# Attention and a gated feed-forward on one core: other planner constants, and the last stores on two queues

## The chip, the core and the metric

The kernel runs on one core of a Trainium2 chip. The time is the device time of one execution in microseconds, given as the median of several runs; a profile is one execution taken by the hardware profiler. Times in the profile count from the start of its span.

## The reference

```python
scores = (1 / sqrt(64)) * q @ k.T                 # q, k, v: 8 batches, 12 heads, 448 rows, 64 columns
attn = exp(scores - max(scores)); attn = attn / (sum(attn) + 1e-9)
x = (attn @ v) as 3584 x 768                      # heads side by side
h = x @ w_in                                      # 768 x 2048
out = (h * sigmoid(h)) @ w_out                    # 2048 x 768, float32
```

## The kernel before

**Stages and names.** The work is in 16-bit floats with float32 sums in PSUM. Heads are taken in groups of four, three groups to a batch. A *unit* is one group with all its queries; in batch 0 each group makes two units of half the queries (224 columns, units 0 to 5), and from batch 1 on there are units 6 to 26 with 448 columns. In the profile the tiles have these names:

- `rk`, `rq`, `V`: keys, queries and values as they are loaded on GpSimd's queue; `KT`, `QT`: transposed by VectorE (lines 285, 296).
- `s`: scores, one *burst* for each quarter of the keys (line 311). A matmul of a burst has 32 rows, so that the four heads run in four row groups of TensorE. A burst fills two PSUM tiles (heads 0 and 1, heads 2 and 3); there are only two such tiles, tag `s`. Units 7 on come in pairs (7 and 8, 9 and 10, ...), whose last quarters share a burst of 16.
- `E`: the exp of the scores on ScalarE (line 348), two instructions to a burst. `T`: sums of E over key quarters on VectorE (line 359), an add that shortens the sums of weights.
- `a`: three products with E for each unit (line 375): part 0, the sums of weights, with `ones`; parts 1 and 2, with `V`. They run in column groups.
- `sT`, `inv`, `rdn`: transpose, reciprocal and spread of the sums of weights on VectorE (lines 415, 421, 424); `xT`: the normalized output (line 432), which is the input x of the feed-forward.
- `h`: x times one of the 16 blocks of w_in (line 446); `th`: tanh on ScalarE (line 457); `G` and `X`: (tanh + 1) times h on VectorE (line 493), the gated values.
- `o`: four plain products with w_out for the first two row tiles (line 551). `p`: all other products with w_out (line 537), as 13 *quads*: two row tiles by two halves of the inner dimension by two halves of the columns, in seven products in place of eight. They need sums of G (`S`, and G itself, line 527), sums of w_out (`D1`, `D4`, `D6` and two written into `w_out_t`, line 483), and sums of the results, read from PSUM by ScalarE copies and VectorE adds (lines 590 to 604, tiles `s`, `m`, `ost`).
- `z`: products of zeros that keep TensorE at work while it waits at the start (line 1148).

The tiles a, h, o, p and z share four PSUM banks, tag `m`: each product holds its bank until what reads it is done (sT for part 0, xT for parts 1 and 2, G for h, copies and adds for o and p).

**What sets the order.** Nothing is left to the compiler. The kernel carries a planner (class `Order`, line 89 on) that steps through a modelled time, with modelled costs of each instruction and counters for buffers (`Ring`), and writes down in which order each engine gets its instructions. ScalarE and VectorE take, of what is ready, the instruction with the least (ready time + bias); the biases are the numbers that stand in each `Op` (-2 for tanh, -1 for the gate, -10 for the sums' inverse, 8 for S, 20 for the transposes of k and q, 100 for the sums of w_out). TensorE chooses in the main loop: a score burst if it can run and either `PACE` modelled microseconds have gone by since the last, or no product of the list `moe` (h, o, p) is ready, or that list has fewer than 6 entries; otherwise a product of the list, otherwise a part of a. The planner's times only give the order; on the chip each engine runs its instructions in that order, each waiting for its inputs by semaphores.

Units 0 to 5 issue each burst as two halves of 8 matmuls, one for each pair of heads (the tuple `split`, line 964).

**Stores.** `store` (line 575) writes an output tile of 128 x 384 with four DMAs of 32 rows. They are issued by SP; only for the last quad (`4 * qd + 4 == NT * B`) and its tiles (0,0) and (1,1) the two odd ones are issued on ScalarE's queue.

Of the kernel before, what the change touches and what calls it, by code (L numbers as in the profile page):

```python
# [164 lines left out]
def kernel(  # L165
# [25 lines left out]
    NDC = DM // 128  # L191
    NT = 2 * S // 128
    OH = DM // 2
    PACE = 3
    LONE = NG + 1
    PIECES = ((0, 7), (7, TPP))
    NE, NXT = 9, 16
# [377 lines left out]
    def store(qd, i, j):  # L575
        u, t = divmod(2 * qd + i, NT)
        for w in range(4):
            r, col = divmod(128 * t + 32 * w, S)
            b = 2 * u + r
            dst = out[b * S : (b + 1) * S, OH * j : OH * (j + 1)].rearrange(  # L580
                "(i g) m -> g i m", g=TPP
            )

            eng = nc.scalar if w % 2 and 4 * qd + 4 == NT * B and i == j else nc.sync
            eng.dma_start(
                out=dst[col // 32], in_=ost_t[(qd, i, j)][32 * w : 32 * (w + 1), :]
            )
# [143 lines left out]
    moe = []  # L731
# [7 lines left out]
    def queue_ffn1(b, g0, g1):  # L739
        t0, t1 = 32 * g0, 32 * g1  # L740
        for f in range(NFF) if b == 0 else [x for f in range(HF) for x in (f, f + HF)]:

            def run(f=f):
                op = Op("PE", NDC * mm(t1 - t0), lambda: ffn1(b, f, t0, t1), tail=PE_OUT)
                if warm["on"]:
                    warm["on"] = False
                    m_ring.give(od.now)
                m_ring.take()
                od.on_pe(op, "full")
                th = od.add(  # L750
                    Op("ACT", act(t1 - t0), lambda: tanh(b, f, t0, t1), [op], -2, tail=0.2, ring=th_ring)
                )
                g = Op(
                    "DVE",
                    (t1 - t0) / 960.0 + 0.13,
                    lambda: gate(b, f, t0, t1),
                    [th],
                    -1,
                    then=lambda at: (m_ring.give(at), th_ring.give(at)),
                )  # L760
                g_op.setdefault((b, f), []).append(od.add(g))
                ffn1_left[b] -= 1

            def deps(f=f):
                made = [(x_op[(b, cc, g0)], cc * mm(t1 - t0)) for cc in range(NDC)] + ld_win[f]

                u, r = divmod(b, 2)
                for qd in range(NT * B // 4) if u else ():
                    if any(t // NT == u - 1 and (r or t % NT < 4) for t in (2 * qd, 2 * qd + 1)):
                        made += (  # L770
                            [plain_op.get(x) for x in ((0, 0), (0, 1), (1, 0), (1, 1))]
                            if qd == 0
                            else [pr_op.get((qd, m)) for m in (3, 4, 6, 7)]
                        )
                return made

            moe.append((deps, 1, run))
            ffn1_left[b] += 1

    def sums_w(ms):  # L780

        for m in ms:
            w_op[m] = [
                od.add(
                    Op(
                        "DVE",
                        0.9,
                        lambda m=m, f0=f0: combine_w(m, f0, f0 + 4),
                        ld_wout[0] + ld_wout[1] + list(plain_op.values()) * (m in (3, 7)),
                        100,  # L790
                    )
                )
                for f0 in (0, 4)
            ]

    def queue_plain(t, j):
        def run():
            op = Op("PE", NFF * mm(OH), lambda: plain(t, j), tail=PE_OUT)
            m_ring.take()
            od.on_pe(op, "full")  # L800
            plain_op[(t, j)] = op
            od.add(
                Op(
                    "ACT",
                    act(OH),
                    lambda: take_plain(t, j),
                    [op],
                    -0.3,
                    then=lambda at: (m_ring.give(at), ost_ring.give(at + STORED)),
                    ring=ost_ring,  # L810
                )
            )
            if len(plain_op) == 4:
                sums_w((3, 7))

        def deps():
            if any(len(g_op.get((0, f), ())) < len(PIECES) for f in range(NFF)):
                return [None]
            return ld_wout[j] + [(x, f * mm(OH)) for f in range(NFF) for x in g_op[(0, f)]]

        moe.append((deps, 1, run))
# [37 lines left out]
    def queue_quad(qd):  # L859
        quads.append(qd)  # L860
        took = {}

        def read(m, eng, fn, deps, *free):
            busy = act(OH) if eng == "ACT" else OH / 960.0 + 0.13
            bias = -0.3 if eng == "ACT" else -1
            ring = tmp_ring[m] if m in tmp_ring else ost_ring if m in (2, 5, 6, 7) else None

            def then(at):
                for r in free:
                    r.give(at)  # L870
                if ring is ost_ring:
                    ring.give(at + STORED)

            took[m] = od.add(Op(eng, busy, lambda: fn(qd), deps, bias, then=then, ring=ring))

        def queue(m, first):
            def run():
                op = Op("PE", HF * mm(OH), lambda: product(qd, m), tail=PE_OUT)
                if BANK[m] == m:
                    m_ring.take()  # L880
                if m in (5, 2, 1):
                    op.then = sg_ring.give
                od.on_pe(op, "full")
                pr_op[(qd, m)] = op
                if m == 3:
                    read(3, "ACT", take_3, [op])
                elif m == 4:
                    read(4, "DVE", take_4, [op, took[3]])
                elif m == 5:
                    read(5, "ACT", take_5, [op], m_ring)  # L890
                elif m == 2:
                    read(2, "ACT", take_2, [op], m_ring)
                elif m == 1:
                    read(1, "DVE", take_1, [op, took[4]])
                    read("less_12", "DVE", less_12, [took[1], took[5]])
                    read("less_21", "DVE", less_21, [took[1], took[2]])
                elif m == 6:
                    read(6, "DVE", take_6, [op, took["less_21"]], m_ring, tmp_ring[1])
                else:
                    read(7, "DVE", take_7, [op, took["less_12"]], m_ring, tmp_ring[3])  # L900

            def deps():
                made = list(w_op.get(m, [None])) + [x for y in first if y for x in [took.get(y)]]
                if m in (3, 4):
                    t = 2 * qd + m - 3
                    for b in {(128 * t + c) // S for c in (0, 127)}:
                        for f in range(HF):
                            x = g_op.get((b, f + HF * (m - 3)), [None])
                            made += [(y, f * mm(OH)) for y in x]
                    return made + ld_wout[0] + ld_wout[1]  # L910
                if m in (1, 6, 7):
                    made += [pr_op.get((qd, x)) for x in ((5, 2) if m == 1 else (1,))]
                x = sg_op.get((qd, m), [None, None])
                return made + [x[0], (x[1], 4 * mm(OH))]

            moe.append((deps, 1 if BANK[m] == m else 0, run))


        for m, first in ((3, ()), (4, (3,)), (5, (3,)), (2, (4,)), (1, ()), (6, ()), (7, (1,))):
            queue(m, first)  # L920
# [40 lines left out]
    qk_seq, av_seq = [], []  # L961
    for ns in jobs:
        if len(ns) == 1:
            split = ((0,), (1,)) if ns[0] < 6 else ((0, 1),)
            qk_seq += [(ns, c, ys) for c in range(NCH // per_burst(ns[0])) for ys in split]
        else:
            qk_seq += [([n], c, (0, 1)) for n in ns for c in range(NCH - 1)]
            qk_seq.append((ns, 3, (0, 1)))
        av_seq += [(ns, part) for part in range(3)]
# [139 lines left out]
    def after_av(n, part, op, nq):  # L1109
        b, hg, g0, g1 = units[n]  # L1110
        if part == 0:
            made = []
            before = ([op] + inv_op[-1:], [], norm_op[-4:])
            for step, busy in enumerate((nq / 960.0 + 0.15, 0.2, nq / 960.0 + 0.15)):
# [2 lines left out]
                    busy,  # L1117
                    lambda step=step: inverse(n, step),
                    made[-1:] + before[step],
                    -10,  # L1120
                )
                made.append(od.add(r))
            made[0].then = m_ring.give
# [29 lines left out]
    while True:  # L1153
# [4 lines left out]
        if od.free["PE"] <= od.now:  # L1158
# [6 lines left out]
                moe_i, moe_next = moe_ready(0)  # L1165
                soon.append(min([x for x in m_ring.free if x>od.now] or [od.now+0.1]))
            if qk is not None and qk <= od.now and (
                od.now >= pace["next"] or moe_i is None or len(moe) < 6
            ):
                u0 = units[qk_seq[0][0][0]]  # L1170
                pace["next"] = min(max(pace["next"], od.now - 4), od.now) + PACE * len(qk_seq[0][2]) / 2
                run_qk()
                od.now, keep = od.free["PE"], od.now
                while (a := av_at()) is not None and a <= od.now:
# [58 lines left out]
```

The softmax here doesn't subtract the row's maximum and nothing guards it: scores larger than these inputs give would overflow.

## Time and profile before

| what | value |
|---|---|
| median of 7 runs | 405.27 us (404.99 to 405.65) |
| profiled execution | 404.76 us, span 403.0 us |
| TensorE (PE) busy | 394.5 us, 98% |
| VectorE (DVE) busy | 299.3 us, 74% |
| ScalarE (ACT) busy | 233.8 us, 58% |
| GpSimd (POOL) busy | 95.9 us, 24% |
| granted TensorE clock | 0.999 |
| start of PE's last product | 395.74 us |

"Busy" adds the time of an engine's instructions. A row of the timeline gives the start, the length, the engine, the line and operation, the tiles as out<-in with their sizes, and the number of instructions merged; in brackets the idle time before it and what ended it. In the list of waits the three numbers are the microseconds in total, the number of waits and the longest. SPq and ACTq are the queues' own instructions, the issuing of DMAs.

### The profile page before, as it was taken

How to read it: one execution, taken by the hardware profiler on the slowest of the kernel's cores; microseconds unless marked ns; L12 is line 12 of the kernel's file. 1: busy time of each engine (PE TensorE's matmuls, PEld its weight loads, DVE VectorE, ACT ScalarE, POOL GpSimd, SP SyncE). 2: the span in 40 equal slices, each digit the busy share in tenths (PEclk: the TensorE clock that was granted, in tenths of full speed). 3: DMA queues.
4: the chain of work that ended last, by engine and by line, in shares of the span. 5: the costliest groups of instructions: out<-in, count | busy, mean ns of one | idle time of the engine just before them, and what ended most of it. 6: DMA issues, size and time to landing. Idle time of an engine off the chain costs nothing.

```text
span 403.0 us, 9442 instructions
## 1 busy us (share of the span) xinstructions
PE 394.5 (98%) x3767; PEld 203.3 (50%) x3767; DVE 299.3 (74%) x646; ACT 233.8 (58%) x360; POOL 95.9 (24%) x175
## 2 busy tenths in 40 slices
PE   8999999999999999999999999999999999999994
PEld 7676754444444444444455444443445444655562
DVE  2555676999979797696788678788698677674763
ACT  3887895796566866545961495764971573224410
POOL 6775383724003415120000630530000000000000
PEclk9999999999999999999999999999999999999999
DMA  7999999967015936392002782642002300131024
GB/s 110 175 166 206 196 135 218 182 85 116 2 45 100 172 50 81 58 172 56 0 2 62 124 144 38 92 88 62 1 21 53 88 0 2 35 81 44 2 49 107
DMA packets 38747, 34.43 MB, mean 85 GB/s; under 512 B 11952, under 2 KB 37936, under 8 KB 38704
## 3 DMA queue, kind: packets, MB, share of 16 engines
q0 software_dynamic: 27952, 22.82, 39.2%
q1 hardware_dynamic: 10560, 10.83, 10.4%
q8 instruction: 29, 0.48, 0.5%
q10 hardware_dynamic: 192, 0.20, 0.2%
q14 instruction: 14, 0.11, 0.1%
HBM read 45.61 MB, written 11.01 MB: 141 GB/s over the span
## 4 chain that ended last, share of the span: by engine, by line
PE 96%; DVE 1%; ACT 1%; issue 0%; ACTq 0%
PE h L446 38%; PE p L537 30%; PE s L311 12%; PE a L375 11%; PE o L551 3%; PE z L1148 2%; ACT E L348 1%; DVE T L359 1%; DVE rdn L424 0%; DVE ost L590 0%; DVE sT L415 0%; DVE G L493 0%; DVE X L493 0%; DVE inv L421 0%; DVE ones L212 0%
## 5 line engine op out<-in xcount | busy, mean ns | idle before, releaser
L348 ACT ACTIVATE E<-s 128x896 f16<-128x896 f32 (+1 forms) x172 | 149.2, 915 | 47.8 <-PE s L311 46.5
L446 PE MATMUL h<-xT,w_in_t 128*128 128x448 f16 (+1 forms) x864 | 157.8, 332 | 0.1
L446 PEld LDWEIGHTS <-w_in_t 128*128 128x128 f16 x864 | 79.2, 98 | 72.6 <-issue 19.8
L457 ACT ACTIVATE th<-h 128x448 f16<-128x448 f32 (+1 forms) x144 | 71.7, 505 | 58.1 <-PE h L446 53.4
L493 DVE SCALAR_TENSOR_TENSOR G<-th,h 128x448 f16<-128x448 f16 (+2 forms) x144 | 74.8, 532 | 35.2 <-ACT th L457 33.3
L250 POOL DMA_DIRECT2D V<-in_v_dram x88 | 48.6, 566 | 127.9 <-PE a L375 104.2
L311 PE MATMUL s<-QT,KT 32*128 32x448 f16 (+4 forms) x864 | 56.4, 340 | 0.4 <-ACT E L348 0.4
L537 PEld LDWEIGHTS <-G 128*128 128x128 f16 x384 | 36.7, 98 | 28.5 <-issue 4.6
L537 PEld LDWEIGHTS <-S 128*128 128x128 f16 x312 | 29.5, 98 | 22.8 <-issue 4.3
L375 PE MATMUL a<-E,V 128*32 128x448 f16 (+3 forms) x864 | 40.3, 334 | 0.0
L537 PE MATMUL p<-D,G 128*128 128x384 f16 x208 | 37.8, 326 | 0.5 <-DVE sT L415 0.5
L537 PE MATMUL p<-w_out_t,S 128*128 128x384 f16 x208 | 36.8, 326 | 0.0
L432 DVE SCALAR_TENSOR_TENSOR xT<-a,rdn 128x448 f16<-128x448 f32 (+1 forms) x54 | 28.7, 561 | 6.7 <-PE a L375 6.2
L537 PE MATMUL p<-w_out_t,G 128*128 128x384 f16 x176 | 31.8, 326 | 0.0
L311 PEld LDWEIGHTS <-KT 32*128 32x128 f16 (+2 forms) x864 | 17.5, 98 | 27.9 <-issue 26.6
L359 DVE TENSOR_TENSOR T<-E,E 128x1792 f16<-128x1792 f16 x20 | 21.7, 1087 | 11.4 <-ACT E L348 11.4
L527 DVE TENSOR_TENSOR S<-G 128x512 f16<-128x512 f16 x70 | 26.5, 417 | 4.3 <-PE p L537 4.2
L375 PEld LDWEIGHTS <-V 128*32 128x32 f16 (+2 forms) x864 | 18.2, 95 | 22.4 <-issue 15.5
L359 DVE TENSOR_TENSOR T<-T,E 128x1792 f16<-128x1792 f16 x20 | 21.7, 1086 | 8.8 <-ACT E L348 8.8
L231 POOL DMA_DIRECT2D rk<-in_k_dram x24 | 13.7, 570 | 38.6 <-DVE KT L285 35.3
L285 DVE STREAM_TRANSPOSE KT<-rk 128x256 f32<-128x256 f32 (+3 forms) x48 | 16.6, 384 | 8.0 <-DMA rk<-in_k_dram 7.1
L600 ACT COPY ost<-p 128x384 f32<-128x384 f32 x13 | 6.3, 482 | 24.4 <-PE p L537 24.4
(41 smaller groups left out, 269.5 us busy)
## 6 DMA issues: line engine op xcount, KB each, us to landing
out_dram<-ost SPq DMA_DIRECT2D x220, 48.0 KB, 1.6
rk<-in_k_dram POOLq DMA_DIRECT2D x24, 224.0 KB, 5.1
rq<-in_q_dram POOLq DMA_DIRECT2D x21, 224.0 KB, 6.1
w_out_t<-in_moe_w_out_dram POOLq DMA_DIRECT2D x8, 384.0 KB, 9.9
V<-in_v_dram POOLq DMA_DIRECT2D x43, 64.0 KB, 4.7
V<-in_v_dram POOLq DMA_DIRECT2D x40, 48.0 KB, 4.5
w_in_t<-in_moe_w_in_dram POOLq DMA_DIRECT2D x16, 96.0 KB, 4.3
w_in_t<-in_moe_w_in_dram POOLq DMA_DIRECT2D x8, 192.0 KB, 7.3
```

Of the source, the lines that this page charges most:

```text
L250: nc.gpsimd.dma_start(out=VT[b][32 * x : 32 * (x + 1), hs, 0:count, :], in_=v[b, hs].rearrange("h (i g) d -> i h g d", g=TPP)[:, :, first ...
L285: nc.vector.transpose(out=turned.rearrange("p c x i -> p x c i")[:, x:y, 0:count], in_=t[:, first : first + count * (y - x)].rearrange("p ...
L311: nc.tensor.matmul(out=pS[p0 : p0 + 32 * (x1 - x0), h % 2, at : at + nq], lhsT=KT[(b, hg)][32 * h : 32 * (h + 1), c, x0:x1, :, e], rhs=QT[ ...
L348: nc.scalar.activation(out=E[(n, w)][0:kr, 2 * y : 2 * y + 2, 0:nk], in_=pS_t[(n, w, y)][0:kr, :, 0:nk], func=AF.Exp, scale=attn_scale,)
L359: nc.vector.tensor_tensor(out=T_t[n], in0=E[(n, 0)] if c == 1 else T_t[n], in1=E[(n, c)], op=ALU.add,)
L375: nc.tensor.matmul(out=a[32 * h : 32 * (h + 1), 0:nq], lhsT=w, rhs=e[k0:k1, h, at : at + nq], start=start, stop=stop,)
L432: nc.vector.scalar_tensor_tensor(out=xT[(b, cc)][:, 32 * g0 : 32 * g1], in0=acc[(n, part)][:, 0:nq], scalar=0.5, in1=rdn_t[n].rearrange("p ...
L446: nc.tensor.matmul(out=h[:, 0 : t1 - t0], lhsT=w_in_t[:, cc, 128 * f : 128 * (f + 1)], rhs=xT[(b, cc)][:, t0:t1], start=(cc == 0), stop=(c ...
L457: nc.scalar.activation(out=th, in_=h_t[(b, f, t0)][:, 0 : t1 - t0], func=AF.Tanh)
L493: nc.vector.scalar_tensor_tensor(out=dst[:, f, at + lo : at + hi], in0=th_t[(b, f, t0)][:, lo - t0 : hi - t0], scalar=1.0, in1=h_t[(b, f, ...
L527: nc.vector.tensor_tensor(out=dst[:, f0:f1], in0=x[:, f0:f1], in1=y[:, f0:f1], op=op)
L537: nc.tensor.matmul(out=pr_t[(qd, BANK[m])][:, 0:OH], lhsT=w[:, f, :], rhs=W_[m][:, f, :], start=(f == 0 and BANK[m] == m), stop=(f == HF - 1),
```

## The change

It changes constants of the planner and one condition of `store`. The pace of scores goes from 3 to 4 and may be made up for over 2 modelled microseconds in place of 4; scores go ahead of the pace whenever fewer than 30 products wait, in place of 6. Units 4 and 5 issue whole bursts. The biases of tanh, gate, the copies and adds that read p and o, the inverse of the sums of weights and the sums of w_out change. All four output tiles of the last quad put their odd stores on ScalarE's queue.

```diff
-    PACE = 3
+    PACE = 4
...
-            eng = nc.scalar if w % 2 and 4 * qd + 4 == NT * B and i == j else nc.sync
+            eng = nc.scalar if w % 2 and 4 * qd + 4 == NT * B else nc.sync
...
-                    Op("ACT", act(t1 - t0), lambda: tanh(b, f, t0, t1), [op], -2, tail=0.2, ring=th_ring)
+                    Op("ACT", act(t1 - t0), lambda: tanh(b, f, t0, t1), [op], -0.3, tail=0.2, ring=th_ring)
...
                     lambda: gate(b, f, t0, t1),
                     [th],
-                    -1,
+                    -4,
...
                         lambda m=m, f0=f0: combine_w(m, f0, f0 + 4),
                         ld_wout[0] + ld_wout[1] + list(plain_op.values()) * (m in (3, 7)),
-                        100,
+                        30,
...
                     lambda: take_plain(t, j),
                     [op],
-                    -0.3,
+                    0.5,
...
-            bias = -0.3 if eng == "ACT" else -1
+            bias = 0.5 if eng == "ACT" else -4
...
-            split = ((0,), (1,)) if ns[0] < 6 else ((0, 1),)
+            split = ((0,), (1,)) if ns[0] < 4 else ((0, 1),)
...
                     lambda step=step: inverse(n, step),
                     made[-1:] + before[step],
-                    -10,
+                    0,
...
-                od.now >= pace["next"] or moe_i is None or len(moe) < 6
+                od.now >= pace["next"] or moe_i is None or len(moe) < 30
...
-                pace["next"] = min(max(pace["next"], od.now - 4), od.now) + PACE * len(qk_seq[0][2]) / 2
+                pace["next"] = min(max(pace["next"], od.now - 2), od.now) + PACE * len(qk_seq[0][2]) / 2
```

## The prediction

> **What bounds the kernel now.** I read the page first, then the waits of PE, the chain that ended last, and the timeline of five stretches. The page says that TensorE is nearly all of the span.
>
> ```profile
> PE 394.5 (98%) x3767; PEld 203.3 (50%) x3767; DVE 299.3 (74%) x646; ACT 233.8 (58%) x360; POOL 95.9 (24%) x175
> PE 96%; DVE 1%; ACT 1%; issue 0%; ACTq 0%
> ```
>
> PE is busy 394.5 of 403.0 us, and 96% of the chain lies on it. An edit pays in three ways only: less PE time, fewer waits of PE, or a shorter stretch after PE's last product. The waits that PE shows are small:
>
> ```profile
> PE z L1148 <- DVE zeros L214: 1.0, 1, 1.0
> PE a L375 <- ACT E L348: 0.6, 1, 0.6
> PE p L537 <- DVE sT L415: 0.5, 1, 0.5
> PE s L311 <- ACT E L348: 0.4, 1, 0.4
> ```
>
> Comparing the time from each PE group to the next with the median of its kind gives the real losses, since a modelled end hides part of a wait: 0.88 us at the weight sums of unit 5 (34.6), 0.17 at the first product after it (37.3), 0.32 and 0.31 where two score bursts stand 2.06 us apart (58.4, 76.1), 0.70 at 178, and 0.11, 0.12, 0.12, 0.20 at 98, 148, 247 and 277. That is 2.9 us.
>
> The second view is the price of a score burst in the first batch. Whole bursts have 16 matmuls; units 0 to 5 issue them as two halves of 8.
>
> ```profile
> 7.71 0.60 PE L311 MATMUL s<-QT,KT 32*128 32x224 f16 x16
> 8.24 0.62 PE L1148 MATMUL z<-zeros 128*128 128x128 f16 x8
> 23.34 0.57 PE L311 MATMUL s<-QT,KT 32*128 32x224 f16 x8
> 23.84 0.57 PE L375 MATMUL a<-E,ones 128*32 128x224 f16 x16
> ```
>
> From start to next start, 16 matmuls on four row groups take 0.53 us (7.71 to 8.24), and 8 matmuls on two row groups take 0.50 (23.34 to 23.84). A half costs as much as a whole.
>
> The third view is the end.
>
> ```profile
> 384.74 16.09 SPq L585 DMA_DIRECT2D out_dram<-ost  x28
> 395.74 1.46 PE L537 MATMUL p<-w_out_t,G 128*128 128x384 f16 x8
> 397.01 1.82 ACTq L585 DMA_DIRECT2D out_dram<-ost  x4
> 397.24 0.56 DVE L590 TENSOR_TENSOR ost<-p,s 128x384 f32<-128x384 f32 x1 [0.26 <-PE p L537]
> ```
>
> The last output tile is made at 397.79, but SP issues stores until 400.83. It issues 20 without a pause from 391.24, one per 0.465 us, except for 0.6 us near 398. SP is late by its own issuing.
>
> **Merged score halves (units 4 and 5): -2.2 us of PE.** The order of the changed program is the same up to 22.67, where the first product h starts; the filler matmuls z are the same 111. From there to the start of the first h of the second piece (37.33) both orders hold the same work, except that 8 half bursts become 4 whole ones. Before, the stretch took 14.66, of which 0.88 was the wait at unit 5: 13.78. After: eight h groups (0.575 each, 0.67 before a change of kind) 5.0, four whole bursts at 0.53 are 2.12, two triples of a at 1.28 are 2.56, and the a groups of unit 5 with one burst of unit 6 are 1.89. Sum 11.57, so 2.2 less.
>
> **Waits that this adds: +1.5 us.** A whole burst needs both PSUM buffers of the scores free, and frees them only after two exps. From a burst's start to its first exp is 0.635 (23.34 to 23.975); two exps take 1.73:
>
> ```profile
> 36.55 1.73 ACT L348 ACTIVATE E<-s 128x896 f16<-128x896 f32 x2 [0.96 <-PE s L311]
> ```
>
> So two whole bursts stand at least 2.38 apart, and more where tanh is queued ahead on ScalarE. Walking the new order with these rows: unit 4's second burst starts at 26.97, a tanh (0.36) holds ScalarE until 27.58, its exps end at 29.33; PE has only two h (1.25) in between and reaches unit 5's first burst at 28.74. Wait 0.6. Unit 5's second burst then starts at 32.37, its exps end at 34.73, and the weight sums behind it want them at 33.0. Before, that wait cost 0.88, and now about 1.7. Another 0.15 comes where h waits for a PSUM bank whose tanh now stands behind exps (43.7). Net of the stretch about -0.7. If exps were no later than before, the wait is +0.7; if every tanh came first, +2.2, and the edit gives nothing.
>
> **Changes of kind elsewhere: -0.25.** Counting in the two orders, PE changes between row-tiled, column-tiled and full products 229 times before and 221 after; six of the eight belong to the merge. With one direct step from a pair's sums to its next part lost, the PE rows of the rest sum to about 0.25 less.
>
> **Waits after 59 us: -0.95.** The biases and the pace only move instructions. The two 0.3 us waits stay: the distances between these bursts are the same. The 0.70 at 178 is this:
>
> ```profile
> 175.73 0.61 DVE L415 STREAM_TRANSPOSE sT<-a 128x448 f32<-128x448 f32 x1
> 176.37 1.09 DVE L359 TENSOR_TENSOR T<-E,E 128x1792 f16<-128x1792 f16 x1
> 178.22 0.61 DVE L415 STREAM_TRANSPOSE sT<-a 128x448 f32<-128x448 f32 x1
> 178.88 1.46 PE L537 MATMUL p<-D,G 128*128 128x384 f16 x8 [0.53 <-DVE sT L415]
> ```
>
> The add T stood between the two sT, whose second frees the bank that p needs. In the new order this pair has one p between its sums and its next part, no T lies between its sT, and the second sT ends some 0.2 us before the bank is wanted. Two products later an add to a store tile stands behind a T, for a wait of about 0.25. The same walk at 98, 247 and 277 finds the wait gone, and at 148 unchanged. So 1.25 of waits become 0.3. What is not in the trace is how VectorE does where scores now stand inside blocks of p (206 to 220 and 300 to 309 before had none): there a score burst and two p give PE 3.2 us and VectorE about 3.0 (two sevenths of a quad's ten sums at 0.335 and seven reads at 0.47, plus two thirds of a T at 1.0). That is cover, but thin. Bounds: -1.25 if nothing is late, +0.5 if two or three waits of 0.7 come in. I take -0.95, near the rows that I walked.
>
> VectorE is full from 76.2 to 107.8 (0.37 us idle), and two weight combinations of 0.9 us move forward into that stretch; in exchange seven half sums of 0.335 move behind the read of the first p. In the new order every bank that PE wants there is free 0.2 to 2 us ahead, so they cost nothing. Without that cover, 1.8.
>
> Loads: GpSimd's order is the same kinds in the same sequence; k for the fourth group lands at 67.4 and its q at 68.8 whatever PE does. Coming 0.7 us earlier, PE still finds QT 0.5 us ahead of its use, and w_out 0.9 ahead.
>
> **Stores of the last quad: -1.75.** Two stores each of tiles (0,1) and (1,0) move from SP to ScalarE's queue. On SP, 16 issues remain after 391.24 instead of 20. Twelve end at 396.8, before tile (1,1) is made (396.98); its two start at 397.03 and 397.5, tile (0,0)'s at 397.96 and, as its completion counter is shared with the store that ScalarE issues at 397.0 (1.65 us to landing, the cause of the 0.6 us pause before), 398.66. Before, the last started at 400.41. The landing and the ending after it are unchanged, so the end moves 1.75. On ScalarE four issues of 0.43 are added; the copy behind the first two waits for PE until 393.3 anyway, and they end at 392.1. Bounds: -2.0 without the shared counter, 0 if the DMA engines and not the issue held the end. The rows are near the first: landing takes 1.6 us for single stores and for the last alike.
>
> The Trainium skill speaks against this edit: "DMA: Bandwidth & Descriptors", section "Issuing engines are not separate DMA queues", says that starting DMAs from several engines saves only the sequencer's issue time, usually small beside the DMA. By that rule the term would be near 0 and the sum -1.9; here 20 issues of 0.465 make 9.3 us against one landing of 1.6, so I expect the row to decide.
>
> **The sum.** -2.2 + 1.5 - 0.25 - 0.95 - 1.75 = -3.65 us, on a span of 403.0: 399.35. The profiled execution took 404.76, 1.76 more than its span and 0.51 under the median of 405.27. Against that median: 401.6.
>
> **Rivals.** (1) The stores give nothing, because the transfers share their engines: -1.9, 403.4. For it: DMA is busy 44% from 397.2 on. Against it: SP is never seen waiting at the end but for the one counter. Chance 0.10. (2) The new order gains nothing on PE: exps and bank waits take back all of the 2.2, and new waits fill the rest. Only the stores are left, -1.75: 403.5. ScalarE is 11.3 of 14.6 us busy in the stretch of the merge, which speaks for it; the walk, in which each wait has its row, speaks against it. Chance 0.09, and 0.06 that both rivals come together and the time stays at 405.3. (3) Slower: VectorE's queue. The wait of 178, a T ahead of what frees a bank, recurs at the pairs, since the sums now rank with the T adds (bias 0 for both). At all ten pairs it costs 7.0 us, 6.3 more than now: -2.7 + 6.3 = +3.6, 408.9. It decides from five or six pairs on. For it: VectorE is 38.8 of 44 us busy from 59 to 103. Against it: in the order I see a T between the sT of no pair. Chance 0.07. (4) The change doesn't do what it says: scores are not spread wider after 200 us. With the pace dropped below 30 waiting products, unit 19's and 20's bursts come inside the p block instead of after it. That is in the walk already and has no price of its own.
>
> **How the numbers follow.** The forecast has 0.68, with 400.5 to 403.2 as its own range: -4.75 with a wait of 1.0 for the merge, no late p and stores at -2.0; -2.1 with a wait of 1.9, one or two new waits of 0.7 and stores as summed. The upper end goes on to 404.0 for rivals 1 and 2, whose own terms can be off by 0.5: 400.5 to 404.0. A measurement of this kernel can tell 0.2%, 0.8 us, from no change. Faster by more are the forecast and each of these rivals alone, 0.68 + 0.10 + 0.09 = 0.87; within it the two together, 0.06; slower rival 3, 0.07.
>
> **What would show it.** In the profile after: whole bursts of 16 at 24 to 33 us; waits of PE on E of about 0.6 and 1.1 shown or more near 29 and 34; the first h of the second piece at 36.5 instead of 37.3; no wait of p on sT near 178; the last product's end about 1.9 us earlier; SP's last issue 0.9 us after the last output tile instead of 2.6. I am wrong if PE shows waits on VectorE of over 2 us together, or if the time from the last output tile to the end stays at 5.2 us.

## The result, and the profile after

The changed kernel takes 401.33 us in the median of 22 runs, against 405.14 of 56 runs of the kernel before; the ratio is 0.9933, with a 95% interval of 0.9912 to 0.9953. In a second series, with five rounds side by side, it is 0.9909 (0.9895 to 0.9923). The forecast was 401.6, within 400.5 to 404.0.

The lines of "after" come from a second profiled execution of the changed kernel, of 402.2 us with a span of 400.4, since the first had a granted clock of 0.50 from 12 to 28 us and took 5.7 us more than the median, as some executions of either kernel do, most of which the ratios and the medians below leave out. At 402.2 it is 1 us above the median of its series (401.22), so its span fell by 2.54 where the median fell by 3.83; the reason is seen below.

The page of the kernel after, busy time and chain:

```profile
PE 392.6 (98%) x3767; PEld 203.2 (51%) x3767; DVE 299.6 (75%) x646; ACT 234.1 (58%) x360; POOL 95.9 (24%) x175
PE 80%; DMA 14%; POOL 3%; SPq 1%; issue 1%; DVE 1%; ACT 0%; POOLq 0%
```

PE still fills the span. New is the 14% of the chain on DMA, which the chain before does not list: in this execution PE reaches points where it waits for a load, and the chain then runs back along the loads. The change alone does not do that: in the first profiled execution of the same kernel DMA has 0% of the chain, and neither of the two waits for loads is there. The waits of PE in the execution shown (in all, how many, the longest):

```profile
PE a L375 <- ACT E L348: 1.2, 2, 0.7
PE z L1148 <- DVE zeros L214: 1.0, 1, 1.0
PE s L311 <- ACT E L348: 0.4, 1, 0.4
PE s L311 <- DVE QT L296: 0.4, 1, 0.4
PE a L375 <- issue: 0.3, 1, 0.3
PE h L446 <- DMA w_in_t<-in_moe_w_in_dram: 0.3, 1, 0.3
```

The wait of p on sT is gone, the one of a on E has doubled, and two waits for loads (QT of a late q, and w_in) are there. The merged bursts, in the timeline (here and below some of its rows, others in between left out):

```profile
29.94 0.75 PE L311 MATMUL s<-QT,KT 32*128 32x224 f16 x16
30.65 1.73 ACT L348 ACTIVATE E<-s 128x896 f16<-128x896 f32 x2
33.15 0.61 PE L311 MATMUL s<-QT,KT 32*96 32x224 f16 x16
33.26 0.36 ACT L457 ACTIVATE th<-h 128x224 f16<-128x224 f32 x1 [0.22 <-PE h L446]
33.80 1.72 ACT L348 ACTIVATE E<-s 96x896 f16<-96x896 f32 x2 [0.18 <-PE s L311]
34.76 0.27 PE L375 MATMUL a<-E,ones 96*32 96x224 f16 x2 [0.69 <-ACT E L348]
35.57 0.37 PE L375 MATMUL a<-E,ones 96*32 96x224 f16 x6 [0.53 <-ACT E L348]
```

Unit 5's second burst goes out at 33.15, its exps run to 35.52, and the weight sums that stand right behind it wait twice. The pair of units 15 and 16, where the 0.70 had been:

```profile
176.05 0.38 PE L375 MATMUL a<-E,ones 64*32 64x448 f16 x8
176.37 1.47 PE L537 MATMUL p<-D,S 128*128 128x384 f16 x8
176.50 0.65 DVE L415 STREAM_TRANSPOSE sT<-a 128x448 f32<-128x448 f32 x1
177.77 1.63 PE L375 MATMUL a<-E,V 128*32 128x448 f16 x32
179.98 0.60 DVE L415 STREAM_TRANSPOSE sT<-a 128x448 f32<-128x448 f32 x1
```

One p stands between the pair's sums and its next part, there is no T behind the first sT, and PE goes through without a gap. The end:

```profile
394.51 3.77 SPq L585 DMA_DIRECT2D out_dram<-ost  x7
394.92 1.46 PE L537 MATMUL p<-w_out_t,G 128*128 128x384 f16 x8
396.19 1.82 ACTq L585 DMA_DIRECT2D out_dram<-ost  x4
396.42 0.56 DVE L590 TENSOR_TENSOR ost<-p,s 128x384 f32<-128x384 f32 x1 [0.26 <-DMA out_dram<-ost]
```

The last tile is made at 396.98 and SP ends its issuing at 398.28, 1.3 behind it and no longer 3.0. From the start of the last product to the end of the span it is 5.50, before it was 7.22.

### The profile page after: what moved, and what is told of

It is laid out like the page before. It is cut to its first block, busy times and chain, and to the rows that moved or that the text cites. A ratio compares the mean times of both kernels' runs of the same rounds, so it can differ in the third digit from the quotient of the medians.

```text
span 405.2 us, 9444 instructions
## 1 busy us (share of the span) xinstructions
PE 398.1 (98%) x3767; PEld 205.6 (51%) x3767; DVE 300.3 (74%) x646; ACT 234.5 (58%) x360; POOL 95.8 (24%) x175
## 4 chain that ended last, share of the span: by engine, by line
PE 95%; ACT 1%; SPq 1%; issue 1%; DMA 0%; DVE 0%; ACTq 0%
PE h L446 36%; PE p L537 28%; PE a L375 13%; PE s L311 13%; PE o L551 3%; PE z L1148 2%; ACT E L348 1%; SPq L585 1%; DMA out_dram<-ost 0%; DVE ost L590 0%; ACT ost L600 0%; DVE G L493 0%; ACT th L457 0%; DVE zeros L214 0%; DVE ones L212 0%
## 5 line engine op out<-in xcount | busy, mean ns | idle before, releaser
L446 PE MATMUL h<-xT,w_in_t 128*128 128x448 f16 (+1 forms) x864 | 156.1, 332 | 0.1
L446 PEld LDWEIGHTS <-w_in_t 128*128 128x128 f16 x864 | 80.3, 98 | 70.3 <-issue 15.2
L311 PE MATMUL s<-QT,KT 32*128 32x448 f16 (+4 forms) x864 | 57.6, 352 | 0.8 <-ACT E L348 0.8
L375 PE MATMUL a<-E,V 128*32 128x448 f16 (+3 forms) x864 | 42.5, 349 | 0.0
L375 PEld LDWEIGHTS <-V 128*32 128x32 f16 (+2 forms) x864 | 19.2, 99 | 23.5 <-issue 16.2
L415 DVE STREAM_TRANSPOSE sT<-a 128x448 f32<-128x448 f32 (+1 forms) x27 | 15.7, 581 | 5.5 <-PE a L375 4.9
```

The lines of the kernel that those rows point to most:

```text
L311: nc.tensor.matmul(out=pS[p0 : p0 + 32 * (x1 - x0), h % 2, at : at + nq], lhsT=KT[(b, hg)][32 * h : 32 * (h + 1), c, x0:x1, :, e], rhs=QT[ ...
L375: nc.tensor.matmul(out=a[32 * h : 32 * (h + 1), 0:nq], lhsT=w, rhs=e[k0:k1, h, at : at + nq], start=start, stop=stop,)
L446: nc.tensor.matmul(out=h[:, 0 : t1 - t0], lhsT=w_in_t[:, cc, 128 * f : 128 * (f + 1)], rhs=xT[(b, cc)][:, t0:t1], start=(cc == 0), stop=(c ...
```

## The experiments

The times are medians; the differences are against the kernel before in the same series (405.05 in the first, 405.15 in the second, 405.24 in the third). "Early" is the stretch from the first product h (near 23) to the first h of the second piece (near 37), "late" the one from the first h of batch 1 (near 76) to the start of the last product, "tail" from there to the end of the span. Before, they are 14.66, 318.86 and 7.22.

| kernel | time, us | difference | ratio, 95% interval | early | late | tail |
|---|---|---|---|---|---|---|
| whole change | 401.22 | -3.83 | 0.9909 (0.9895 to 0.9923) | 13.83 | 317.47 | 5.50 |
| stores only | 403.40 | -1.65 | 0.9973 (0.9931 to 1.0015) | - | 318.85 | 5.50 |
| all but the stores | 403.37 | -1.68 | 0.9978 (0.9953 to 1.0003) | 13.83 | 317.38 | 7.20 |
| merge only | 404.26 | -0.79 | 0.9989 (0.9955 to 1.0024) | 13.83 | 318.84 | 7.27 |
| planner constants only | 404.25 | -0.90 | 0.9977 (0.9952 to 1.0003) | - | 317.37 | 7.23 |
| old pace | 403.16 | -2.08 | 0.9961 (0.9910 to 1.0012) | 13.83 | 319.26 | 5.51 |
| old biases | 401.29 | -3.95 | 0.9884 (0.9829 to 0.9940) | 13.82 | 317.79 | 5.51 |
| unit 5 in halves | 401.10 | -4.05 | 0.9889 (0.9849 to 0.9929) | 13.14 | 317.47 | 5.52 |
| 128-row stores | 406.18 | +1.03 | 1.0036 (1.0005 to 1.0066) | 13.83 | 317.37 | 10.56 |
| 64-row stores | 413.35 | +8.20 | 1.0213 (1.0155 to 1.0272) | - | - | 17.82 |
| unit 5 in halves, two quads on two queues | 400.51 | -4.73 | 0.9875 (0.9818 to 0.9933) | 13.16 | 317.45 | 5.41 |

A dash stands where the early rows can't be compared or the stretch is not needed. Several ratios alone can't be told from 1; the stretches, which agree within 0.1 us between kernels with the same order, carry the argument. Each stretch is read from one execution.

**The three parts: stores, merge, planner.** The whole change again:

> The changed kernel again, for a profile at full clock. The prediction's sum: 3.65 us less than the kernel before, 2.2 less by merged halves, 1.5 more by waits on exps in the same stretch (first h of the second piece at 36.5 us), 0.25 less by fewer changes of kind, 0.95 less by waits after 59 us, 1.75 less at the end (from the last output tile to the end of the span 3.45 us in place of 5.2). Rival (stores give nothing): 1.9 less. Rival (only the stores give): 1.75 less.

Only the stores, in the kernel before:

```diff
-            eng = nc.scalar if w % 2 and 4 * qd + 4 == NT * B and i == j else nc.sync
+            eng = nc.scalar if w % 2 and 4 * qd + 4 == NT * B else nc.sync
```

> The kernel before with the store edit alone; the order of PE, VectorE and GpSimd is that of before. If SP's issuing held the end: 1.75 us less (bounds 1.3 and 2.0), the last issue at 398.7 in place of 400.4. If the transfers held it: within 0.2 us of before.

The changed kernel with that line as before:

> The changed kernel without the store edit. By the sum 1.9 us less than before, and 1.75 more than the changed kernel; if the stores give nothing, the same as the changed kernel; if the order on PE gives nothing, the same as before.

Only the merge, in the kernel before:

```diff
-            split = ((0,), (1,)) if ns[0] < 6 else ((0, 1),)
+            split = ((0,), (1,)) if ns[0] < 4 else ((0, 1),)
```

> The kernel before with whole bursts for units 4 and 5 alone. By the prediction's walk 2.2 us of PE less, of which 1.5 come back as waits on exps before the first h of the second piece: 0.7 less (36.6 us for that h, 37.3 before); the wait of 0.7 near 178 can stay or go, as the planner shifts what follows. If exps are covered: 1.5 to 2.2 less. If ScalarE takes all back: within 0.2.

Measured: -1.65 for the stores alone, -1.68 without them, -0.79 for the merge alone. The stores show only in the tail (7.22 to 5.50), the merge only in the early stretch (14.66 to 13.83). With the merge alone the wait at 178 is still in the list of waits of PE:

```profile
PE p L537 <- DVE sT L415: 0.5, 1, 0.5
```

So the late gain belongs to neither; it comes with the planner's constants. -1.65 and -1.68 add to -3.33 of the -3.83; the 0.5 that is missing is within the scatter of these medians, as the runs behind the -1.68 reach from 402.75 to 407.41.

**The constants without merge and stores.** The changed kernel with both conditions as before:

> All the planner's constants as changed, but units 4 and 5 still in halves and the last stores as before. By the sum of the prediction only the changes of kind and the waits after 59 us are left: -0.25 - 0.95 = -1.2 us against the kernel before. If the parts add up as measured so far (no store edit -1.68, merge alone -0.79), it is -0.9. A rival: with these constants the planner puts second halves straight beside first halves of the next burst (unit 4's second with its next first, and so on), where two halves on different row groups run side by side as one whole does. Then this order gets most of the gain of the merge without it: the stretch from the first product h to the first h of the second piece falls from 14.66 to 13 or less by itself, and the kernel is 2 us or more faster than before.

It measured -0.90: the sum of parts. The late stretch is 317.37, the full gain of 1.5, so the part before it gives 0.6 back. Rows of PE in its profile, whose granted clock is 0.50 from 20 to 28 us:

```profile
27.16 1.20 PE L446 MATMUL h<-xT,w_in_t 128*128 128x224 f16 x6
41.39 2.47 PE L446 MATMUL h<-xT,w_in_t 128*128 128x224 f16 x24
59.61 0.73 PE L446 MATMUL h<-xT,w_in_t 128*128 128x224 f16 x6 [1.03 <-DVE G L493]
64.30 0.57 PE L311 MATMUL s<-QT,KT 32*128 32x448 f16 x6 [0.43 <-ACT E L348]
```

The first h starts at 27.16 and the first h of the second piece at 41.39, 14.23 later. The first h is 0.46 longer at this clock, and one burst more than before (0.50) stands ahead of the second piece; without both it is 13.3, an estimate, against 14.66 before. So these constants shorten the early stretch even without the merge, near to what the rival said. But then a product h waits 1.0 for G, and a score burst near 64, in two parts, 0.8 for E. Counted to the first h of batch 1, and without the 0.46, it is 54.81 against 54.21 before. In the time the rival, 2 us or more, is refuted: halves in this order do not replace the merge, with which the same constants give -1.68. Why the waits at 59 to 64 come was not tried.

**Pace or biases.** The changed kernel with the old pace, and with the old biases:

```diff
-    PACE = 4
+    PACE = 3
...
-                od.now >= pace["next"] or moe_i is None or len(moe) < 30
+                od.now >= pace["next"] or moe_i is None or len(moe) < 6
...
-                pace["next"] = min(max(pace["next"], od.now - 2), od.now) + PACE * len(qk_seq[0][2]) / 2
+                pace["next"] = min(max(pace["next"], od.now - 4), od.now) + PACE * len(qk_seq[0][2]) / 2
```

> The changed kernel with the pace of the scores as before (3, 4 and 6 in place of 4, 2 and 30), all biases changed. TensorE changes between kinds of product 227 times, against 221 in the changed kernel and 229 before. If the pace made the gain of 1.4 to 1.5 us between the first product h of batch 1 and the last product (318.86 before, 317.4 after), this stretch is 318.3 or more. If the biases made it: 317.6 or less. The wait of 0.7 at the pair of units 15 and 16: a T lies between its two sT again, but five products instead of none stand between its sums and its next part, so no wait.

```diff
-                    Op("ACT", act(t1 - t0), lambda: tanh(b, f, t0, t1), [op], -0.3, tail=0.2, ring=th_ring)
+                    Op("ACT", act(t1 - t0), lambda: tanh(b, f, t0, t1), [op], -2, tail=0.2, ring=th_ring)
...
                     made[-1:] + before[step],
-                    0,
+                    -10,
```

and so on for the gate, the reads of p and o, and the sums of w_out.

> The changed kernel with all biases as before, the pace changed. TensorE changes kinds 221 times, as in the changed kernel, and no T lies between two sT. If the pace makes the gain: 317.4 to 317.7 from the first h of batch 1 to the last product, and the time within 0.4 us of the changed kernel. If the biases are needed for VectorE to keep up (gates and reads of p first): waits on G, sT or s come back, 318.3 or more.

With the old biases the late stretch is 317.79 and the time 401.29, that of the whole change. With the old pace it is 319.26, longer than before (318.86). So the new pace alone brings 1.07 of the 1.39 to 1.48; the new biases bring the other 0.3 to 0.4, but only beside it, since with the old pace they cost 0.4. The 317.79 lies just above the 317.7 expected, and in the time the biases can't be told from nothing. The expectation of "no wait" at units 15 and 16 with the old pace failed. With the old pace, in the timeline:

```profile
182.68 0.56 DVE L590 TENSOR_TENSOR ost<-p,s 128x384 f32<-128x384 f32 x1 [2.06 <-DMA out_dram<-ost]
183.29 1.06 PE L375 MATMUL a<-E,V 128*32 128x448 f16 x20 [0.32 <-DVE ost L590]
204.64 0.57 PE L311 MATMUL s<-QT,KT 32*128 32x448 f16 x6 [0.27 <-ACT E L348]
```

VectorE stood 2.06 us before a store tile, until an older store had landed, and the bank that a wanted stayed taken, which cost PE 0.60 from group to group; 0.64 more went at a score burst (204.0) that stood 1.78 behind the one before. These are two waits of one execution.

**The price of whole bursts.** The changed kernel, unit 5 in halves again:

```diff
-            split = ((0,), (1,)) if ns[0] < 4 else ((0, 1),)
+            split = ((0,), (1,)) if ns[0] < 4 or ns[0] == 5 else ((0, 1),)
```

> The changed kernel with unit 4 whole and unit 5 in halves again. The waits that the merge added (0.5 to 0.6 at unit 5's first burst, 1.68 at its sums of weights) are put down to whole bursts that need two exps. If so, both shrink: 0 to 0.2 and 0.2 to 0.6. Against that stand about 0.5 for one more half that runs alone and 0.15 for changes of kind. Net about -0.6 against the changed kernel in the stretch to the first h of the second piece (13.83 becomes about 13.2). Rival: ScalarE, with 11.3 us of work in this stretch, sets its length, and waits come back elsewhere: 0.

The early stretch went from 13.83 to 13.14, as expected. In the timeline of this kernel:

```profile
33.48 0.93 ACT L348 ACTIVATE E<-s 96x896 f16<-96x896 f32 x1
34.46 0.37 PE L375 MATMUL a<-E,ones 96*32 96x224 f16 x6 [0.20 <-ACT E L348]
```

The sums of unit 5 wait for one exp and no longer for two: 0.46 in place of 1.67, counted from group to group, and the wait at unit 5's first burst is gone (the h ahead of it took 0.38 longer than its kind, as in the profile after). So the added waits at the sums are those of bursts that need two exps. In the time, 401.10 against 401.22, it can't be told from nothing: in this execution later waits, for q and others, took 0.4 and more back. From the first h to the first h of batch 1 the same order of PE took 53.69 here, and 52.74 in the last kernel of the table. That the difference is when loads land is argued from the waits, not tried.

**Fewer, larger stores.** The changed kernel, with one DMA on SP for each of the last four tiles:

```diff
+        if 4 * qd + 4 == NT * B:
+            g0 = (128 * t - S) // 32
...
+            nc.sync.dma_start(out=dst[g0 : g0 + 4], in_=ost_t[(qd, i, j)])
+            return
```

> The changed kernel, but each of the last four output tiles is stored by one DMA of 128 rows on SP (192 KB) instead of four of 32 rows on two queues: 4 issues instead of 16. If issuing holds the end, SP's last issue starts at the last tile instead of 0.9 us behind it: the time from the last product's start to the end of the span falls from 5.50 to 4.6, -0.9. If a transfer of 192 KB takes longer to land than one of 48 KB by its bytes (the last stretch moves up to 230 GB/s, so 0.64 for the 144 KB more), the gain is 0.3. If the transfers and not the issues held the end all along, the time is the same or later.

And with two of 64 rows, one on each queue:

> As the kernel with one DMA to a tile, but two DMAs of 64 rows for each of the last four tiles, one on SP and one on ScalarE's queue: 8 issues. Both last issues start at the last tile. If issuing holds the end: -0.9 against the changed kernel, as with one DMA. If the bytes of one DMA count, 96 KB lands 0.2 later than 48 KB: -0.7. If a shared completion counter holds the last issue back again by 0.5: -0.4.

Both failed by far: +5.0 and +12.1 against the changed kernel, all of it in the tail (10.56 and 17.82 in place of 5.50). That the kernel with 128-row stores could be later was among the theories, but none had the reason or the size. The busy time by microsecond with 128-row stores (the last three columns are PE's clock, the share of the 16 DMA engines, and GB/s):

```profile
398.00:399.00 1.00, 0.00 (x0) 0.00 (x0) 0.00 (x0) 0.00 (x0) 0.00 (x0) 1.00 0.28 100
399.00:400.00 1.00, 0.00 (x0) 0.00 (x0) 0.00 (x0) 0.00 (x0) 0.00 (x0) 1.00 0.26 98
401.00:402.00 1.00, 0.00 (x0) 0.00 (x0) 0.00 (x0) 0.00 (x0) 0.00 (x0) 0.50 0.26 95
```

and with 64-row stores:

```profile
404.00:406.00 2.00, 0.00 (x0) 0.00 (x0) 0.00 (x0) 0.00 (x0) 0.00 (x0) 0.50 0.13 47
406.00:408.00 2.00, 0.00 (x0) 0.00 (x0) 0.00 (x0) 0.00 (x0) 0.00 (x0) 0.50 0.13 51
```

Issuing had ended by 396.56 and 401.15; what follows is transfer, at 0.26 and 0.13 of the engines: 4 and 2 of 16. The destination of these DMAs is [4, 32, 384] and [2, 32, 384], that of the 32-row stores [32, 384]; those move 206 GB/s at 0.87 of the engines near 397.5 in the changed kernel. The Trainium skill says why in "DMA: Bandwidth & Descriptors", section "Why a DMA increments its semaphore by 16 and not by 1": a DMA runs on the largest number of engines, up to 16, that divides the outermost dimension of both its sides. The shares agree, 4/16 = 0.25 and 2/16 = 0.125. So the four small stores to a tile are no waste: their outermost dimension is 32. One DMA of the same 128 rows with 32 outermost was not tried.

**The shared counter.** The kernel with unit 5 in halves, and the odd stores of two quads on ScalarE's queue:

```diff
-            eng = nc.scalar if w % 2 and 4 * qd + 4 == NT * B else nc.sync
+            eng = nc.scalar if w % 2 and 4 * qd + 8 >= NT * B else nc.sync
```

> The kernel with unit 5 in halves, and now the odd stores of the last eight output tiles (two quads) on ScalarE's queue, not only of the last four. By issuing alone it should give nothing: SP's queue is empty when the last quad's tiles come. But the completion counters then alternate strictly between the two queues, so that SP's last store no longer waits for a counter that ScalarE's store of the tile before still holds (0.54 us of pause on SP before the last issue at 397.97 in the changed kernel). If that counter costs the time: from the last product's start to the end 5.05 instead of 5.50. If the DMA engines hold the end (87% busy in the microsecond before the last issue): 5.50 as before. If the four more issues on ScalarE make its copies late: more than 5.50.

The tail is 5.41, near the second theory: the pause is gone, but it brings 0.09 and not 0.45. In the timeline of this kernel:

```profile
388.84 7.47 SPq L585 DMA_DIRECT2D out_dram<-ost  x12
392.23 4.18 ACTq L585 DMA_DIRECT2D out_dram<-ost  x6
394.83 0.56 DVE L590 TENSOR_TENSOR ost<-p,s 128x384 f32<-128x384 f32 x1 [0.26 <-PE p L537]
```

SP ends 0.92 behind the last tile (396.31 against 395.39) and not 1.3, but now ScalarE's last store is the last to land: issued at 395.97, landed at 397.75, 1.78 us, where SP's take 1.53 to 1.68. In the changed kernel ScalarE's last store had landed at 399.23, only 0.27 ahead of SP's at 399.50. So the counter could never give more than that, and with both queues issuing at once the DMA engines are 0.90 busy in the last full microsecond of stores. This kernel, 400.51, is the fastest that was run, and its interval overlaps that of the whole change.

## Why the prediction was right

**The sum** was -3.65, the medians say -3.8. Its terms, each at its place:

- **Merged halves, -2.2 of PE work, and waits, +1.5.** Net -0.7 was forecast, with a wait of 0.15 in it that lies behind the early stretch; in this stretch -0.83 was measured, in every kernel of the table that has both units merged. In the kernel without the store edit the two waits are 0.59 and 1.68, against 0.6 and 1.7; the stretch without them is 13.83 - 2.27 = 11.56, against 11.57. In the whole change the first wait shows as 0.15, after 0.44 from group to group for a late w_in: the load took its place, and the sum stayed. The wait for a bank near 43.7 was 0.17 against 0.15.
- **Changes of kind, -0.25, and waits after 59 us, -0.95.** Together -1.2 was forecast, -1.48 measured without the store edit (318.86 to 317.38). The waits that were counted, 0.70, 0.19, 0.12, 0.12 and 0.11, are down to one of 0.11: -1.13, against -0.95, since the wait of 0.25 that was foreseen two products behind units 15 and 16 did not come. The rest, -0.35, is put down to the work, and was not tried by itself. The two waits of 0.3 stayed, as said. The prediction left open which constant does it: the pace does 1.07, the biases beside it 0.3 to 0.4.
- **Stores, -1.75.** -1.72 was measured in the tail, -1.65 in the time. The Trainium skill's sentence in "DMA: Bandwidth & Descriptors", section "Issuing engines are not separate DMA queues", that starting DMAs on several engines saves only the time to start them, agrees with what was saved here: four issues of 0.465 us off SP's queue. That this is usually small did not hold while SP still had issues in a row behind the last tile; behind the change, four more issues on the other queue brought 0.09.
- **What was not in the sum: loads.** "Coming 0.7 us earlier, PE still finds QT 0.5 us ahead" was wrong in some executions. In nine profiles with the same order of PE ahead of it, the first h starts between 22.63 and 23.50. The fourth load of V, issued at 8.63 to 9.07, lands there at 15.45 to 16.50, and where it is late PE's products with V go on 0.09 behind it (at 16.59 after 16.50 in the kernel with the merge only, at 15.72 after 15.63 in the one with the old biases). The profile after has 0.46 of wait for QT near 71 and 0.44 for w_in at 28.3. This explains why this one profile gained 2.54: start +0.76, early -0.83, from there to batch 1 +0.64, late -1.39, tail -1.72. For the same reason two signs that the prediction named are not in this profile: the first h of the second piece is at 37.26 and not at 36.5, and the last product is 0.82 earlier and not 1.9. In the kernel without the store edit they are 36.76 and 1.97.

The three stretches alone add to -4.03 (-0.83, -1.48, -1.72). The medians say 0.2 less, which is less than what the start moves.

**The rivals.** That the stores give nothing is refuted by the tail; that only they give something, by the 0.83 and 1.48. That T before sT recurs at the pairs did not come: no wait of PE on sT is left. That scores are not spread wider: with the old pace PE changes kinds 227 times, with the new one 221, so the pace does change the order, and this is where the late gain is.

## What to carry to other kernels

When one engine is full, walk the new order group by group with durations from the trace before: each wait added or removed had its row, and the terms held to 0.3 us. Look at the queue behind the last output: a store that is issued late costs as much as a late product, and a second queue helps until both land together. Before joining DMAs, look at the outermost dimension of both sides: four stores of 32 rows beat one of 128, as the one ran on 4 of 16 engines.

## What was not expected of the hardware

- A store of 128 x 384 floats with the destination [4, 32, 384] moves 95 to 100 GB/s at a DMA share of 0.26 to 0.28; with [2, 32, 384] and 64 rows 47 to 51 GB/s at 0.13; 32-row stores reach 206 GB/s at 0.87.
- In the kernel with two quads on two queues, stores issued at the same time on both land 1.53 to 1.68 us after the issue on SP and 1.74 to 1.87 on ScalarE's.
- Loads issued in the same order land at different times from one execution to the next: the fourth of V 6.65 to 7.66 us after its issue over nine profiles. Where PE waits for them this moves what follows, the first h by up to 0.87.
